# Copies out of the transposes' PSUM banks moved ahead in the engines' queues of an attention and FFN kernel

## The chip, the cores and the metric

The kernel runs on one core of a Trainium2 chip. The metric is the device time of one execution in microseconds (us). Times are medians over several runs; a 95% interval is given where two kernels are compared. Engine names are those of the profile: PE is TensorE's matmuls, PEld its weight loads, DVE is VectorE, ACT is ScalarE, POOL is GpSimd, SP is SyncE. PSUM is the memory that the matmuls and transposes write; its parts are called banks.

## The reference

Attention with a threshold, then an RMS-norm and a gated feed-forward network (FFN). B=8, H=8, S=576, D=64, so 4608 tokens of width 512; d_ff is 1536.

```python
scores = (1/8) * q @ k.T
thresh = scores.max(-1) - tau                     # tau = 0.02
scores = where(scores >= thresh, scores, -1e9)
attn   = softmax(scores)
x      = (attn @ v)                               # heads side by side: 4608 x 512
xn     = x / sqrt(mean(x*x) + 1e-6) * rms_g
out    = (silu(xn @ w_gate) * (xn @ w_val)) @ w_out
```

## The kernel before

The program builds a list of operations and sorts it itself. Each operation has an engine, an assumed cost, a priority number, the operations it depends on, and the PSUM banks it takes or frees. `order_ops` simulates the engines with the assumed costs and fixes the order of every engine's queue when the kernel is built. Among the ready operations of an engine the earliest goes first, and among equals the one with the lower priority number, so **a lower number goes ahead**.

```python
def order_ops(ops, ring_sizes):
    ...
        for e, lst in pending.items():
            ...
            for i in lst:
                o = ops[i]
                t = max(t0, ready_at[i])
                if o.ring is not None:          # banks: wait until o.nring are free
                    free = [f for f in ring_free[o.ring] if ...]
                    if len(free) < o.nring:
                        continue
                    t = max(t, sorted(free)[o.nring - 1][0])
                ...
                k = (t + (BIAS if other else 0.0), o.prio, i)
                if cand is None or k < cand:
                    cand = k
    ...
    seq = order_ops(ops, {"R": 4})
```

Four PSUM banks form the ring `R`. FFN products, attention products and all transposes take their banks from it. A transpose of K and Q (28 sets, two banks each) is emptied by one DVE copy and one ACT copy. Seven transposes of K tails take one bank each, emptied by ACT and then DVE. Four transposes of the last query rows, or query tails, take two banks, both emptied by ACT.

```python
    t = gated(add("PE", COST["tr_qk"], -500.0, ..., tr, ring="R", nring=2, mode=1), prio)
    for r, rs in enumerate(HALF):
        def ev(o, r=r, rs=rs):
            src = ring[t.slot[r]].rearrange("p (j c n) -> p j c n", j=2, n=64)
            if EVAC[r] == "ACT":
                nc.scalar.copy(out=dst[:, :, :, rs], in_=src)
            else:
                nc.vector.tensor_copy(out=dst[:, :, :, rs], in_=src)
        done.append(add(EVAC[r], COST["evac_qk"], prio, [t], ev, frees=(t, r)))
```

What the moved DVE copies pass is the softmax read: it takes the scores of one step out of PSUM (`s_ps`), with the row's extreme. The next score step's matmuls may overwrite `s_ps` only after it. There are 144 score steps, each with two reads of about 0.75 us.

```python
    # the score step: 8 or 16 matmuls into s_ps, waits for the two reads of step s - 1
    for h in range(2):
        deps.append(ttr_of.get((s - 1, h)))
    o = add("PE", COST["s_main" ...], s, deps, fn, ...)

    # the softmax reads of step s
    for h in range(2):
        def ttr(o, h=h):
            nc.vector.tensor_tensor_reduce(
                out=ssb[a][:, h], in0=s_ps[h][:, ROW_AT:ROW_AT + S], in1=zrow, scale=-1.0 / 8.0, scalar=3.0e38,
                op0=ALU.add, op1=ALU.min, accum_out=mx[m][:, h:h + 1])
        ttr_of[s, h] = add("DVE", COST["ttr"], s - 1, [so, o_c] + exp_of.get(s - NSS, []), ttr)
```

FFN blocks are four matmuls `gmm` or `vmm` (gate or value product) that need a bank of the ring, but no softmax result of the score steps around them. They fill PE while the softmax of a step is under way.

## Time and profile before

| | before |
|---|---|
| time, median of the first 3 runs | 564.16 us (564.16 to 564.22) |
| span of the profiled run | 562.9 us |
| PE busy | 553.0 us, 98% |
| ACT, DVE, POOL busy | 459.9, 425.5, 322.5 us |
| granted clock | 0.998, full but for the end |
| ACT copy of K/Q starts after its transposes' end | 1.76 us on average, at most 5.98 |
| DVE copy of K/Q, same | 1.11 us, at most 1.71 |
| ACT copies of query tails, same | 2.21 us, at most 3.41 |

The last three rows are read from the timeline: for every transpose block, the start of its copies less the end of the block. They show what the change goes for: a bank with finished data stands for 1 to 2 us while the copy waits in its queue.

### The profile page before, as it was taken

The numbers are of one execution on the slowest core, as the hardware profiler recorded it, in microseconds if no ns is written. First come the engines' busy times: TensorE is split into PE (matmuls) and PEld (weight loads), VectorE is DVE, ScalarE is ACT, GpSimd is POOL, SyncE is SP. The second block draws the span as 40 slices with busy tenths as digits, with TensorE's granted clock in tenths as the row PEclk, the third lists the DMA queues.
The fourth block names the chain that finished last, engine by engine and source line by source line (L and its number), as shares of the span: only waits on it lengthen the run. The fifth ranks groups of instructions, "written<-read, shape, count | busy, mean of one in ns | idle before, by whom it ended". The sixth has DMA issues, their size and how long they took to land.

```text
span 562.9 us, 15217 instructions
## 1 busy us (share of the span) xinstructions
PE 553.0 (98%) x5768; PEld 315.7 (56%) x5768; DVE 425.5 (76%) x1091; ACT 459.9 (82%) x741; POOL 322.5 (57%) x462
## 2 busy tenths in 40 slices
PE   8899999999999999999999999999999999999997
PEld 4656766757767555545555455545555444444674
DVE  4889987869968589658885889578966886596354
ACT  5999998998989788879888997888989988885332
POOL 2378946985767456665667666666666664551000
PEclk9999999999999999999999999999999999999999
DMA  8999999979986498889887799988898544662210
GB/s 189 259 283 271 159 191 192 193 145 187 202 184 115 111 178 156 181 161 186 151 175 174 122 168 179 181 179 157 171 189 178 116 95 92 151 95 52 85 39 37
DMA packets 270025, 89.08 MB, mean 158 GB/s; under 512 B 252544, under 2 KB 262272, under 8 KB 269952
## 3 DMA queue, kind: packets, MB, share of 16 engines
q1 hardware_dynamic: 267168, 86.02, 75.8%
q0 software_dynamic: 1600, 1.57, 1.8%
q8 instruction: 45, 0.74, 0.6%
q10 hardware_dynamic: 1184, 0.52, 0.3%
q14 instruction: 28, 0.23, 0.2%
HBM read 37.75 MB, written 9.44 MB: 84 GB/s over the span
## 4 chain that ended last, share of the span: by engine, by line
PE 94%; DVE 2%; ACT 1%; DMA 1%; issue 1%; POOL 0%; SPq 0%; DVEq 0%
PE s_ps L569 30%; PE ring L795 17%; PE ring L800 16%; PE ring L856 15%; PE ring L700 6%; PE ring L304 2%; PE ring L696 2%; DVE ssb L592 1%; PE ring L662 1%; PE s_ps L800 1%; PE s_ps L834 1%; PE s_ps L856 1%; DMA stage<-in_q_dram 1%; PE ring L365 1%; PE s_ps L795 0%
## 5 line engine op out<-in xcount | busy, mean ns | idle before, releaser
L592 DVE CUSTOM_DVE_ANT_0 ssb<-s_ps,zrow 128x576 f32<-128x576 f32 x288 | 207.1, 752 | 64.4 <-PE s_ps L569 46.5
L610 ACT ACTIVATE ssb<-ssb,nth 128x576 f32<-128x576 f32 x224 | 166.1, 767 | 27.5 <-POOL nth L599 27.1
L569 PE MATMUL s_ps<-qkt 64*64 64x288 f32 (+1 forms) x1792 | 165.9, 417 | 1.5 <-DVE mx L592 1.5
L643 POOL TENSOR_SCALAR wsb<-ssb,nth 128x576 f16<-128x576 f32 x64 | 110.5, 1726 | 9.7 <-DMA wt<-wsb 3.2
L795 PE MATMUL ring<-xnT,wg 128*128 128x256 f16 (+1 forms) x564 | 114.4, 325 | 0.3 <-DVE xsb L718 0.3
L569 PEld LDWEIGHTS s_ps<-qkt 64*64 64x64 f32 (+1 forms) x1792 | 78.1, 140 | 62.5 <-DVE mx L592 15.5
L800 PE MATMUL ring<-xnT,wv 128*128 128x512 f16 (+1 forms) x528 | 110.4, 331 | 0.0
L599 POOL TENSOR_SCALAR nth<-mx 128x2 f32<-128x2 f32 x144 | 31.7, 220 | 128.1 <-DVE mx L592 118.0
L812 DVE SCALAR_TENSOR_TENSOR sl<-th,ring 128x256 f32<-128x256 f32 (+1 forms) x141 | 77.0, 546 | 30.9 <-ACT th L809 29.6
L617 ACT ACTIVATE wsb<-ssb 128x1152 f16<-128x1152 f32 x80 | 93.0, 1162 | 4.3 <-DMA wt<-wsb 2.2
L809 ACT ACTIVATE th<-ring 128x256 f32<-128x256 f32 (+1 forms) x141 | 67.5, 480 | 29.7 <-PE ring L795 24.7
L856 PE MATMUL ring<-wo,hf 128*128 128x512 f16 x384 | 90.0, 380 | 0.0
L648 POOL TENSOR_TENSOR wsb<-wsb,esb 128x576 f16<-128x576 f16 x64 | 81.8, 1279 | 10.3 <-ACT esb L629 6.0
L817 DVE TENSOR_TENSOR hf<-ring,sl 128x512 f16<-128x512 f32 (+1 forms) x132 | 74.9, 567 | 9.3 <-PE ring L800 0.5
L800 PEld LDWEIGHTS <-wv 128*128 128x128 f16 x576 | 52.2, 98 | 44.5 <-issue 14.2
L795 PEld LDWEIGHTS <-wg 128*128 128x128 f16 x576 | 52.0, 98 | 42.2 <-issue 12.2
L856 PEld LDWEIGHTS <-hf 128*128 128x128 f16 x408 | 37.3, 98 | 47.0 <-issue 7.0
L629 ACT ACTIVATE esb<-ssb,nth 128x576 f16<-128x576 f32 x64 | 49.2, 769 | 6.1 <-POOL nth L599 5.8
L700 PE MATMUL ring<-va,wt 128*128 128x65 f16 (+1 forms) x1264 | 53.0, 193 | 0.0
L700 PEld LDWEIGHTS <-wt 128*128 128x128 f16 (+1 forms) x1280 | 48.8, 100 | 3.8 <-issue 0.7
L614 ACT ACTIVATE wsb<-ssb 128x576 f16<-128x576 f32 x64 | 43.6, 681 | 1.6
L696 PE MATMUL ring<-va,wt 128*128 128x130 f16 (+1 forms) x158 | 35.2, 227 | 0.6 <-ACT qTv L473 0.6
(68 smaller groups left out, 442.3 us busy)
## 6 DMA issues: line engine op xcount, KB each, us to landing
vst<-in_v_dram SPq DMA_DIRECT2D x32, 256.0 KB, 3.7
qkn<-in_k_dram SPq DMA_DIRECT2D x31, 256.0 KB, 3.8
out_dram<-osb SPq DMA_DIRECT2D x31, 256.0 KB, 2.8
qkn<-in_q_dram SPq DMA_DIRECT2D x28, 256.0 KB, 4.3
stage<-in_moe_w_gate_dram SPq DMA_DIRECT2D x6, 512.0 KB, 5.9
stage<-in_moe_w_val_dram SPq DMA_DIRECT2D x6, 512.0 KB, 6.5
wt<-wsb SPq DMA_TRANSPOSE x128, 3.3
wo<-in_moe_w_out_dram POOLq DMA_DIRECT2D x4, 384.0 KB, 6.6
```

The costliest lines, as they stand in the source:

```text
L569: nc.tensor.matmul(s_ps[h][rows, ROW_AT + n * part:ROW_AT + n * part + n], lhs(hs), kT[i][p][h][hs, n * part:n * part + n], start=True, st ...
L592: nc.vector.tensor_tensor_reduce(out=ssb[a][:, h], in0=s_ps[h][:, ROW_AT:ROW_AT + S], in1=zrow, scale=-1.0 / 8.0, scalar=3.0e38, op0=ALU.a ...
L610: nc.scalar.activation(out=ssb[a][:, h], in_=ssb[a][:, h], func=PRELU, scale=-1.0, bias=nth[m][:, h:h + 1], **PRELU_KW)
L617: nc.scalar.activation(out=wsb[s % NW], in_=ssb[a], func=AF.Exp)
L643: nc.gpsimd.tensor_scalar(out=wsb[s % NW][:, h], in0=ssb[a][:, h], scalar1=nth[m][:, h:h + 1], scalar2=None, op0=ALU.is_le)
L648: nc.gpsimd.tensor_tensor(out=wsb[s % NW][:, h], in0=wsb[s % NW][:, h], in1=esb[es], op=ALU.mult)
L700: nc.tensor.matmul(ring[o.slot[0]][rs, at:at + D + 1], w[:, 5 * h + j, rs], va[vi][:, p, 2 * j + h], start=False, stop=(h == 1 and j == 3))
L795: nc.tensor.matmul(ring[o.slot[0]][:, 0:n], wg[d][:, fs], xnT[slot][:, d, 0:n], start=(d == 0), stop=(d == 3))
L800: nc.tensor.matmul(ring[o.slot[0]][:, 0:n], wv[d][:, fs], xnT[slot][:, d, 0:n], start=(d == 0), stop=(d == 3))
L812: nc.vector.scalar_tensor_tensor(out=sl[i][:, 0:n], in0=th[i][:, 0:n], scalar=1.0, in1=ring[g.slot[0]][:, 0:n], op0=ALU.add, op1=ALU.mult)
L817: nc.vector.tensor_tensor(out=hf[hi][:, 0:n], in0=ring[vv.slot[0]][:, 0:n], in1=sl[i][:, 0:n], op=ALU.mult)
L856: nc.tensor.matmul(ring[(first or o).slot[0]], hf[hs[fc][0]][:, 128 * j:128 * (j + 1)], wo[:, fc], start=(fc == 0), stop=(fc == NFC - 1))
```

## The change

Its intent is to give the banks back sooner. The copies' priority numbers go down by 5, 5 and 20 steps, and the first of the two query-tail copies goes from ACT to DVE. No instruction is added or removed. As the priorities feed a list scheduler, any engine's order may come out different, and the changed bank times are among its inputs.

```diff
-            done.append(add(EVAC[r], COST["evac_qk"], prio, [t], ev, frees=(t, r)))
+            done.append(add(EVAC[r], COST["evac_qk"], prio - EVP[0], [t], ev, frees=(t, r)))
...
-            kts.append(add("DVE" if h else "ACT", COST["evac_kt"], prio, [t] + kts, ev, ...))
+            kts.append(add("DVE" if h else "ACT", COST["evac_kt"], prio - EVP[1], [t] + kts, ev, ...))
...
-                nc.scalar.copy(out=qTv[i % 2][:, :, rs],
-                               in_=ring[t.slot[r]][:, 0:64 * NP].rearrange("p (a n) -> p a n", n=64))
+                copy = nc.vector.tensor_copy if not r else nc.scalar.copy
+                copy(out=qTv[i % 2][:, :, rs],
+                     in_=ring[t.slot[r]][:, 0:64 * NP].rearrange("p (a n) -> p a n", n=64))
-            qv_ready[i].append(add("ACT", COST["evac_half"], prio, [t], ev, frees=(t, r)))
+            qv_ready[i].append(add("ACT" if r else "DVE", COST["evac_half"], prio - EVP[2], [t], ev, frees=(t, r)))
...
+EVP = (5.0, 5.0, 20.0)
```

More of the change, by code (lines that the diff above doesn't have):

```diff
@@ L452, in ev @@
                      in_=ring[t.slot[0]][HALF[h], 0:64 * NP].rearrange("p (a n) -> p a n", n=TAIL))
-            kts.append(add("DVE" if h else "ACT", COST["evac_kt"], prio, [t] + kts, ev, frees=(t, 0) if h else None))
+            kts.append(add("DVE" if h else "ACT", COST["evac_kt"], prio - EVP[1], [t] + kts, ev, frees=(t, 0) if h else None))
         for p in range(NP):
```

## The prediction

> **What bounds the kernel now.** I read the page first (busy shares, granted clock), then the busy time by stretch, then the chain of waits in an early and a late stretch, then the waits of TensorE (PE), and last the timeline around every transpose whose copies the change moves.
>
> From the page, and from the table of stretches (columns: stretch, its length, busy us and instructions of each engine, granted clock, DMA share, GB/s):
>
> ```profile
> PE 553.0 (98%) x5768; PEld 315.7 (56%) x5768; DVE 425.5 (76%) x1091; ACT 459.9 (82%) x741; POOL 322.5 (57%) x462
> PEclk9999999999999999999999999999999999999999
> ...
> 14.00:50.00 36.00, 33.43 (x443) 21.91 (x444) 31.74 (x88) 33.21 (x46) 22.21 (x43) 1.00 1.05 272
> 50.00:75.00 25.00, 25.00 (x312) 17.39 (x306) 23.64 (x69) 23.85 (x41) 18.74 (x31) 1.00 1.15 196
> 75.00:150.00 75.00, 74.66 (x935) 48.76 (x930) 60.74 (x172) 67.33 (x117) 52.32 (x71) 1.00 0.97 182
> 150.00:510.00 360.00, 359.43 (x3677) 190.15 (x3674) 277.01 (x684) 310.40 (x486) 224.60 (x304) 1.00 0.79 154
> ```
>
> TensorE is busy nearly always at the full clock. From 150 to 510 us it is busy 359.43 of 360.00 us, with VectorE (DVE) at 77% and ScalarE (ACT) at 86%. Before 75 us DVE and ACT are both close to full as well: 31.74 and 33.21 of 36.00 us, then 23.64 and 23.85 of 25.00.
>
> "Busy" hides slow matmuls, so I checked the pace. In the chain of waits (start us, us, what) a score step, 16 matmuls of L569, looks like this, first early, then late:
>
> ```profile
> 36.65 0.67 DVE ssb L592
> 37.33 0.73 DVE wt L671 x2
> 38.06 0.60 DVE qkt L317
> 38.67 0.08 issue
> 38.75 0.76 DVE ssb L592
> ...
> 42.99 1.87 PE s_ps L569 x16
> ...
> 453.05 1.13 PE s_ps L569 x16
> 454.18 0.97 PE ring L795 x4
> 455.15 0.86 PE ring L800 x4
> 456.01 1.13 PE s_ps L569 x16
> ```
>
> Late, the chain is only TensorE, each score step takes 1.13 us and each FFN block of four 512-column products 0.86, which is 0.216 us a product, back to back. Early, the chain runs through the DVE's softmax reads (L592), its copies of transposed weights (L671) and of transposed K and Q (L317), and a score step stretches to 1.87 us because its second half waits for the reads of the step before.
>
> From the timeline I took for each block of PE instructions the time to the next block's start and subtracted the tenth percentile of blocks of the same kind and successor. The excess, the time in which TensorE is really held up, sums to 15.0 us of 562.9: 0.9 before 14 us, 8.8 from 14 to 75, 3.2 from 75 to 150, 1.5 from 150 to 230, 0.6 from 230 to 510, and nothing in the last 53 us, where the order is FFN work alone. So about 548 us of the span is PE work at its pace. The change leaves that work as it is, and the largest gain that any reordering of copies could have is some 15 us (2.7%), nearly all of it before 230 us.
>
> **What the Trainium skill says.** "PSUM — Partial Sum Buffer", section "Engine vs sequencer instructions", says that the queues of ScalarE and VectorE are strict FIFO. The trace agrees: after the transposes that end at 36.95 us the ACT copy starts 4.43 us later, behind six other ACT instructions, although its data were there. The same page's summary of rules says to evacuate promptly because PSUM is tight; here four banks form the ring that FFN products, attention products and transposes share, and a K/Q transpose holds two. "Perfetto Trace Analysis", section "Identifying the Most-Contended Engine", warns that matmul busy time is not a good measure of the distance to the limit; hence the check of the pace above, which here confirms it after 230 us and refutes it before 75. "VectorE: DVE Perf Modes", section "Why PSUM operands drop a tier", caps fp32 copies from PSUM at one element per cycle, at 0.96 GHz (same page, "Specifications"): 512 elements need at least 0.53 us by it; the trace has 0.685 (L317), and ACT does the same copy in 0.567 (L315).
>
> **The change part by part.** The kernel's order of instructions per engine is fixed at build time by a list scheduler; a lower number goes first among the ready ones of an engine. No instruction is added or removed.
>
> 1. K/Q copies, 28 on DVE and 28 on ACT, move 5 steps forward. In the timeline of before, the DVE copy starts 1.11 us on average after its transposes' end, nearly always behind the two softmax reads (0.75 each); the ACT copy 1.76 us after, at worst 5.98. With 5 steps of lead they go ahead of the reads and exponentials of the current steps. Each pair of banks should come free roughly 0.8 us sooner on DVE (1.11 less about 0.3 for the instruction in hand) and 1.3 on ACT.
> 2. Copies of the K tails, 7 on ACT (0.35) and 7 on DVE (0.43): started 1.32 and 2.40 us after their transposes; both should start within about 0.5 (the DVE one still follows the ACT one).
> 3. Copies of the last query rows: 8 on ACT, 0.36 each, two in a row, started 2.21 us after on average. Four go to DVE at about 0.43 (the duration of the same width in L451). ACT loses 4 x 0.36 = 1.4 us, DVE gains 1.7: too little of 460 and 426 to matter. The pair ends within about 0.8 us instead of 2.6.
>
> What of this lies on the path: only places where PE stood still for such a bank. The waits of PE and the timeline show three.
>
> ```profile
> PE ring L696 <- ACT qTv L473: 0.6, 1, 0.6
> ...
> PE ring L662 <- DVE qkt L317: 0.4, 1, 0.4
> PE ring L795 <- DVE xsb L718: 0.3, 1, 0.3
> ...
> 173.08 0.76 ACT L629 ACTIVATE esb<-ssb,nth 128x576 f16<-128x576 f32 x1
> 173.32 0.10 PEld L696 LDWEIGHTS <-wt 128*128 128x128 f16 x1
> 173.74 0.63 ACT L473 COPY qTv<-ring 128x256 f32<-128x256 f32 x2
> 174.16 0.22 PE L696 MATMUL ring<-va,wt 128*128 128x130 f16 x1 [0.57 <-ACT qTv L473]
> ```
>
> At 174.16 an attention product with its weights loaded waits for the first query-tail copy; at 26.99 a transpose waits for a K/Q copy; at 76.70, with both query-tail banks still held by ACT, an FFN product waits for the one bank left. By the excess of their blocks these cost 0.74, 0.57 and 0.46 us: 1.8 together, and I count all of it as gained.
>
> The other side: a DVE copy ahead of the softmax reads delays them by 0.685, and the next score step waits for those reads. Where FFN blocks can fill, PE loses nothing. Before 50 us there are none: four K/Q transposes and one K tail lie there, so at most 4 x 0.685 + 0.43 = 3.2 us. But the same copy was already on the DVE part of the chain there, only later (38.06 above), so most of it is a swap; I charge a third, 1.1 us.
>
> Third, between 75 and 230 us (4.7 us of excess) free banks let the scheduler put an FFN block where a score step used to follow at once and wait. I count a fifth, 0.9. Sum: -1.8 + 1.1 - 0.9 = -1.6 us, and 564.2 becomes 562.6.
>
> **The rivals.** (a) *Nothing moves*: the held banks are hidden by other work, as PE has no excess from 230 to 510 us although the ACT copy at 295.82 starts 4.06 us late. This speaks for the late part and makes 564. (b) *The delayed softmax becomes the bound*: the scores' reads, then POOL's threshold, then ACT's exponentials all shift by 0.7 to 1.3 us at each of some 13 transposes before 150 us. For it: DVE at 88% and ACT at 92% before 50 us. Against it: later there is filler, and the 20 steps' lead of these inputs is untouched. Charged in full it costs 3.2 before 50 us and perhaps 2 after: 566 to 568. (c) *The banks were the hidden limit early*: free banks let transposes and FFN start sooner and half of the 13.5 us of excess between 14 and 230 us goes: 557. Against it: most of that excess is in score steps that wait for DVE reads, not for a bank.
>
> **Range and chances.** The late 360 us are PE work at full pace and repeat within 0.1 us, so the spread comes from a reshuffled early order: 560.0 to 566.0. Over 2% faster means below 552.9, three quarters of all excess: 0.02. Over 2% slower means 11 us of new stalls in a schedule that has 15: 0.02. Within 2%: 0.96.
>
> **What would show it right or wrong.** The PE wait on L473 at the query tails gone; K/Q copies within about 0.5 us of their transposes on both engines; late score steps still 1.13 us; the busy time from 150 to 510 us of PE unchanged; the score steps before 50 us no longer than now. I am wrong if early score steps lengthen past 1.87 us or PE idles in the waits for L592 more than now (b), if the early stretch shortens by several us (c), or if PE's late order gains switches between its tile shapes and so more work.

## The result and the profile after

The changed kernel takes 564.26 us (563.96 to 565.02, four runs); before, in the same rounds, took 564.19 us (564.16 to 564.23, four runs). The ratio is 1.0003 with a 95% interval of 0.9986 to 1.0021: the same. Ratios here and below are the mean time of one kernel's fast runs over that of the other's of the same rounds, so not quite the ratio of the medians quoted. The profiled spans are 562.3 us after and 562.9 before.

Lines after 473 of the program have moved by one: the score step is now L570, its reads L593, the FFN products L796 and L801, the query-tail copies L474.

The page of the changed kernel: busy us, share and count of each engine.

```profile
PE 550.1 (98%) x5760; PEld 315.2 (56%) x5760; DVE 427.7 (76%) x1095; ACT 458.4 (82%) x737; POOL 322.4 (57%) x462
```

DVE has gained 2.2 us and ACT lost 1.5, mostly the four copies that changed engine. (The eight PE records fewer are of score steps and missing from the trace; no instruction is gone.) PE is busy 2.9 us less, but the span is only 0.6 us shorter. The next view shows where, by stretch, with the columns of the prediction's first fence.

```profile
14.00:50.00 36.00, 32.71 (x440) 22.07 (x438) 31.68 (x90) 32.70 (x46) 21.84 (x43) 1.00 1.08 273
50.00:75.00 25.00, 24.50 (x304) 16.99 (x301) 23.34 (x67) 23.66 (x40) 19.45 (x31) 1.00 1.12 205
75.00:150.00 75.00, 74.04 (x933) 49.70 (x933) 61.24 (x173) 67.35 (x117) 51.92 (x70) 1.00 0.93 173
150.00:510.00 360.00, 359.21 (x3630) 188.62 (x3632) 277.90 (x680) 304.74 (x476) 219.65 (x298) 1.00 0.78 152
```

PE has gaps of 0.7, 0.5, 0.6 and 0.2 us more than before in these four stretches; what it waits for comes below. From 150 to 510 us there are fewer PE instructions in the same busy time (3630 against 3677), and ACT has 5.7 us less to do there: attention's small matmuls and exponentials have moved later, and larger FFN products have come forward. The last softmax read ends at 516.0 us, against 507.0 before, and 960 of the FFN's 1152 first-layer matmuls (four make a block) have begun before it, against 920. The order of work on PE is a different one.

The chain of waits in a late stretch (start us, us, what) answers to the prediction's second fence:

```profile
440.06 1.13 PE s_ps L570 x16
441.19 0.97 PE ring L796 x4
442.16 0.86 PE ring L801 x4
```

The pieces are what they were: 1.13, 0.97 and 0.86 us. The waits of PE (who waited for whom, total us, times, longest):

```profile
PE ring L663 <- ACT wsb L618: 2.4, 3, 1.6
...
PE ring L796 <- DMA xnT<-xn: 0.6, 1, 0.6
PE s_ps L570 <- DVE mx L593: 0.5, 2, 0.3
...
PE ring L801 <- DVE qkt L317: 0.4, 1, 0.4
...
PE ring L796 <- DVE qkt L317: 0.3, 1, 0.3
PE ring L801 <- ACT qkt L315: 0.2, 1, 0.2
```

No wait for a query-tail copy is left. The largest entry is new: at 34.63, 47.92 and 50.93 us (0.32, 1.59 and 0.50 us) the transposes of attention weights wait for ACT's exponentials, a wait that before does not have. It is 2.4 of the 3.8 us that PE stands from 14 to 75 us. FFN products now wait for K/Q copies in three places, although the copies come sooner, because FFN blocks now stand right behind transposes. One wait is for the FFN's own input, `xnT`: at 478.79 us FFN work has run so far ahead that its transposed input has not landed. And in the timeline, at the query tail of 172 us (start us, us, engine, line, operation):

```profile
171.75 0.41 PE L463 MATMUL ring<-id,qtl 64*128 64x64 f32 x8
...
172.19 0.42 DVE L474 COPY qTv<-ring 128x256 f32<-128x256 f32 x1
172.23 0.37 ACT L474 COPY qTv<-ring 128x256 f32<-128x256 f32 x1
```

The two copies now run side by side and end 0.45 us after the transposes (172.61 less 172.16). The change does to the copies what it was meant to: mean delays are 0.37 us on DVE and 0.34 on ACT for K/Q, and 0.32 and 0.25 for the query tails.

**A finer measure.** For the comparison below I took again, for each block of PE instructions, the time from its start to the next block's start, and subtracted the tenth percentile of blocks of the same kind and successor. This time the percentiles are pooled over four kernels: before, after and two experiments, x3_hoist and z1_act_only, which come below. The sum of the percentiles is "work", the rest "excess"; together they fall 7.6 to 7.8 us short of the span in all four kernels. With pooling, the excess of before is 18.1 us instead of the prediction's 15.0.

| us | work | excess | of it 0-14 | 14-75 | 75-150 | 150-230 | from 230 |
|---|---|---|---|---|---|---|---|
| before | 537.2 | 18.1 | 2.6 | 9.4 | 3.4 | 1.6 | 1.1 |
| after | 537.1 | 17.4 | 2.0 | 9.5 | 3.3 | 0.9 | 1.7 |
| x3_hoist | 537.1 | 24.4 | 2.5 | 9.7 | 5.1 | 3.5 | 3.7 |
| z1_act_only | 537.2 | 18.2 | 2.7 | 9.1 | 3.4 | 1.9 | 1.1 |

PE's work has not changed, and neither has its excess, but for a few tenths that come and go. So the new waits for exponentials before 51 us stand in place of other losses there: the net from 14 to 75 us is 0.1.

### The profile page after: what moved, and what is told of

Read it like the earlier page. It is cut to its first block, busy times and chain, and to the rows that moved or that the text cites. A ratio compares the mean times of both kernels' runs of the same rounds, so it can differ in the third digit from the quotient of the medians.

```text
span 562.3 us, 15189 instructions
## 1 busy us (share of the span) xinstructions
PE 550.1 (98%) x5760; PEld 315.2 (56%) x5760; DVE 427.7 (76%) x1095; ACT 458.4 (82%) x737; POOL 322.4 (57%) x462
## 4 chain that ended last, share of the span: by engine, by line
PE 86%; DVE 4%; ACT 3%; DMA 2%; issue 2%; POOL 1%; SPq 1%; DVEq 0%; POOLq 0%
PE s_ps L570 26%; PE ring L801 17%; PE ring L796 17%; PE ring L857 14%; PE ring L701 6%; DVE ssb L593 2%; PE ring L304 2%; PE ring L697 2%; ACT ssb L611 1%; PE s_ps L835 1%; PE s_ps L857 1%; DMA qkn<-in_q_dram 1%; DMA qkn<-in_k_dram 1%; DMA xnT<-xn 1%; PE ring L663 1%
## 5 line engine op out<-in xcount | busy, mean ns | idle before, releaser
L593 DVE CUSTOM_DVE_ANT_0 ssb<-s_ps,zrow 128x576 f32<-128x576 f32 x288 | 208.6, 752 | 71.9 <-PE s_ps L570 56.0
L570 PE MATMUL s_ps<-qkt 64*64 64x288 f32 (+1 forms) x1784 | 163.1, 417 | 0.7 <-DVE mx L593 0.5
L796 PE MATMUL ring<-xnT,wg 128*128 128x512 f16 (+1 forms) x552 | 113.9, 329 | 1.2 <-DMA xnT<-xn 0.6
L801 PE MATMUL ring<-xnT,wv 128*128 128x512 f16 (+1 forms) x552 | 113.8, 329 | 0.6 <-DVE qkt L317 0.4
L570 PEld LDWEIGHTS s_ps<-qkt 64*64 64x64 f32 (+1 forms) x1784 | 77.3, 140 | 59.4 <-issue 14.1
L813 DVE SCALAR_TENSOR_TENSOR sl<-th,ring 128x512 f32<-128x512 f32 (+1 forms) x138 | 76.6, 555 | 19.2 <-ACT th L810 18.0
L810 ACT ACTIVATE th<-ring 128x512 f32<-128x512 f32 (+1 forms) x138 | 67.1, 487 | 26.2 <-PE ring L796 23.4
L818 DVE TENSOR_TENSOR hf<-ring,sl 128x512 f16<-128x512 f32 (+1 forms) x138 | 77.6, 562 | 11.7 <-DVE sl L813 0.9
L801 PEld LDWEIGHTS <-wv 128*128 128x128 f16 x576 | 53.0, 98 | 42.5 <-issue 12.1
L796 PEld LDWEIGHTS <-wg 128*128 128x128 f16 x576 | 51.6, 98 | 44.2 <-issue 13.5
```

Of the source, the lines that this page charges most:

```text
L570: nc.tensor.matmul(s_ps[h][rows, ROW_AT + n * part:ROW_AT + n * part + n], lhs(hs), kT[i][p][h][hs, n * part:n * part + n], start=True, st ...
L593: nc.vector.tensor_tensor_reduce(out=ssb[a][:, h], in0=s_ps[h][:, ROW_AT:ROW_AT + S], in1=zrow, scale=-1.0 / 8.0, scalar=3.0e38, op0=ALU.a ...
L796: nc.tensor.matmul(ring[o.slot[0]][:, 0:n], wg[d][:, fs], xnT[slot][:, d, 0:n], start=(d == 0), stop=(d == 3))
L801: nc.tensor.matmul(ring[o.slot[0]][:, 0:n], wv[d][:, fs], xnT[slot][:, d, 0:n], start=(d == 0), stop=(d == 3))
L813: nc.vector.scalar_tensor_tensor(out=sl[i][:, 0:n], in0=th[i][:, 0:n], scalar=1.0, in1=ring[g.slot[0]][:, 0:n], op0=ALU.add, op1=ALU.mult)
L818: nc.vector.tensor_tensor(out=hf[hi][:, 0:n], in0=ring[vv.slot[0]][:, 0:n], in1=sl[i][:, 0:n], op=ALU.mult)
```

## The experiments

The copies start a microsecond sooner at 39 transposes, and the time stays. Two theories stood at first. **H (hidden)**: the banks were hardly wanted by anyone, so nothing gained and nothing lost. **C (cancel)**: the earlier copies cost something, and something else of about the same size is won. The first four runs do one part of the change, or its opposite.

**e1_qk_only**: only the K/Q copies go ahead; query tails stay on ACT.

```diff
-EVP = (5.0, 5.0, 20.0)
+EVP = (5.0, 0.0, 0.0)
-            qv_ready[i].append(add("ACT" if r else "DVE", ...))
+            qv_ready[i].append(add("ACT", ...))             # and nc.scalar.copy for both
```

> Only the 56 K/Q copies go ahead by 5 steps; K tails and query tails as before. Theory A (TensorE's fixed work sets the time, banks were hidden): within 1 us of 564.2. Theory B (two effects of 1 to 3 us cancel: copies ahead of the softmax cost time early, query tails on two engines win it back): 565 to 567 here, with the loss between 14 and 75 us.

Measured: 573.64 us (571.34 to 575.97) against 564.76, ratio 1.0156 (1.0119 to 1.0193). Slower by 9 us, so H can't be all. Part of it is the clock. The four runs order themselves by it: 571.34 us at a mean granted clock of 1.000, 573.34 at 0.997, 573.93 at 0.996 and 575.97 at 0.994. The stretches of its trace around the dip (columns as above; the third number from the end, ahead of the DMA share, is the granted clock):

```profile
78.00:83.00 5.00, 3.47 (x58) 2.36 (x50) 3.15 (x10) 4.64 (x9) 1.77 (x4) 1.00 0.83 151
83.00:87.00 4.00, 4.00 (x40) 2.10 (x37) 2.33 (x7) 2.52 (x6) 3.67 (x5) 0.57 1.25 244
```

PE stood 1.53 of 5 us, in three waits: 0.38 us at 80.45 for a bank, 0.42 at 81.47 for a late query-tail copy and 0.73 at 82.66 for a DMA of attention weights. From 83.14 us it had half the clock for 3.41 us, which costs about half of that, 1.7 us. That the waits caused it is not shown, as no run takes them away alone. The run at full clock is still 6.6 us slower; where some of that lies comes under y1_qk_and_qt.

**e3_qt_only**: only the query tails, on two engines.

```diff
-EVP = (5.0, 5.0, 20.0)
+EVP = (0.0, 0.0, 20.0)
```

> Only the 8 copies of the last query rows: on two engines, 20 steps ahead. Theory A: within 1 us of 564.2, the wait of PE on the query-tail copy (0.57 us at 174 us) gone, at most 0.7 us gained. Theory B: 562 to 563.

Measured: 563.44 us (562.81 to 563.54) against 564.76, ratio 0.9974 (0.9959 to 0.9989). PE's wait of 0.57 us for the query tail is gone in its trace, and no other has come. This is the one kernel whose interval lies below 1, by 1.3 us in the medians.

**e4_behind**: the opposite, every one of these copies 5 steps later, query tails on ACT.

```diff
+EVP = (-5.0, -5.0, -5.0)
```

> The other way: all these copies go 5 steps behind instead of ahead, so banks stay held longer (1 to 3 us more per transpose). Theory A (banks are hidden by other work after 75 us): under 2 us slower, 564 to 566. Rival C (banks are the hidden limit, and the kernel before already sat where it no longer shows): 4 us or more slower.

Measured: 569.95 us (568.78 to 571.61), ratio 1.0094 (1.0075 to 1.0114). The ACT copies of K/Q started 2.73 us after their transposes on average (1.76 before), at worst 11.2; those of K tails started 3.6 and 4.8 us late, at worst 15 to 16, and those of query tails 5.0. So the opposite of the change costs some 5 us. Whether the longer held banks cost it or the new order that came with them is not shown, as no run delays the copies in a fixed order. By a pooling of its own, about half lies in PE's work and half in excess between 50 and 150 us.

**e6_later_batches**: as after, but the copies of the first two batches (numbers 0 and 1) as before.

```diff
-            done.append(add(EVAC[r], COST["evac_qk"], prio - EVP[0], ...))
+            done.append(add(EVAC[r], COST["evac_qk"], prio - (EVP[0] if b > 1 else 0.0), ...))   # K tails alike
```

> The change, except that batch 1, whose transposes lie before 50 us, keeps its old order. Theory A: within 1 us of 564.2 again. Theory B: the early loss is gone and the query tails' gain stays: 561.5 to 563.

Measured: 563.96 us, ratio 1.0001 (0.9973 to 1.0030; one run took 567.42 at a clock of 0.996). The early copies, on which the prediction spent its charge, make no difference that these runs show.

**How much does a new order do by itself?** A part of the change, like the change, lets the scheduler make a new order. Two runs measure what a meaningless reshuffle does: the scheduler's assumed cost of one operation goes from 800 to 810, which changes no instruction and puts most rows of PE's queue elsewhere.

```diff
-    ... sq=800.0, ...
+    ... sq=810.0, ...
```

**n2_null** is this on before, **n4_null** on after.

> A null change to the kernel before: the scheduler is told that one ACT instruction, the square of the norm, takes 810 ns, not 800; the instructions are the same and no priority changes, but the order of most PE rows does. Theory D: differs from before by up to several us in either direction (2 to 8 us), as e1 and e4 do. Theories A and B, where priorities of copies are what matters: within 1 us of before.

> The same null change to the changed kernel. Theory D: differs from the changed kernel by several us; a spread of 562 to 572 among orders. Theories A and B: within 1 us of the changed kernel, 564.3.

Measured: n2_null 563.39 us against 564.20, ratio 0.9985 (0.9968 to 1.0001); n4_null 564.10, ratio 0.9997 (0.9982 to 1.0012). These two reshuffles moved the time by 0.8 and, against after in other rounds, 0.2 us. The 6.6 us and more of e1 and the 5 of e4 are well outside that, though two reshuffles are a small sample, and e3's gain of 1.3 us is barely larger than what a meaningless edit gave.

**Copies early, everything else in place.** To part the copies from the new order, the schedule of before is kept and the copies alone are moved forward afterwards in their own queues, to where their transposes' data are ready in the scheduler's model.

**x1_hoist** and **x2_hoist_two** (the second with the first query-tail copy on DVE):

```diff
+    for c, t in early:
+        seq.remove(c)
+        ready = max(d.end for d in c.deps) + SEM
+        at = seq.index(t) + 1
+        while at < len(seq) and not (seq[at].eng == c.eng and seq[at].start >= ready):
+            at += 1
+        seq.insert(at, c)
```

> The schedule of before is kept: PE, POOL and DMA queues in exactly the order of before; only the copies (K/Q, K tails, query tails, the last still both on ACT) are taken forward in the DVE and ACT queues to where their transposes end. Theory A (banks cost 1.8 us at three places and an early softmax delay of about 1 us is paid): 562.5 to 565, copies start under 0.6 us after their transposes. Theory D (what moves the time by several us in e1 and e4 is not the copies but the new order that the scheduler makes of everything else): also within 1.5 us of before. Theory B (copies ahead of the softmax cost several us): 567 or more.

> As x1, and the first of each two query-tail copies on DVE: the whole change without a new plan. Theory A: as the changed kernel, 562.5 to 565, the wait at 174 us gone. Theory D: within 1.5 us of x1 and of before.

Measured: 571.66 and 573.0 us, but both gave **wrong results** (relative error 0.478). The loop could put a copy behind its old place, past the next use of its bank. Their times say nothing. The mended version never goes past the old place:

**x3_hoist**, with the query tails on ACT, and **x4_hoist_two**, with the first of them on DVE:

```diff
+    for c, t in early:                  # (copy, its transposes), noted where the copies are added
+        was = seq.index(c)
+        ready = max(d.end for d in c.deps) + SEM
+        at = seq.index(t) + 1
+        while at < was and seq[at].start < ready:
+            at += 1
+        seq.pop(was)
+        c.start, c.end = ready, ready + c.cost
+        seq.insert(at, c)
```

> x1 mended (there a copy could land later than it had been, behind a reuse of its bank, hence the wrong result; both x1 and x2 say nothing on time). PE, POOL and DMA queues in the order of before; the copies only ever move forward, to where their transposes end, the query tails' both on ACT. Theory A (copies as such are worth little either way): 562.5 to 566, copies start under 0.7 us after their transposes on average. Theory B (copies ahead of the softmax cost several us): 567 or more. If it is near before, the 9 us of e1 come from the order that was planned around the copies, not from the copies.

> x2 mended: as x3, with the first of each two query-tail copies on DVE; the whole change, without a new plan of everything else. Theory A: within 1 us of x3 and at most 0.7 us better, as the wait at 174 us goes. If the plan is what the change is worth, x4 is slower than the changed kernel (564.3) by 0.5 us or more; if the copies are, equal to it.

Measured: x3_hoist 570.98 us (570.80 to 571.38) against 564.63, ratio 1.0111 (1.0096 to 1.0126), with right results; x4_hoist_two 571.99, ratio 1.0128 (1.0113 to 1.0143). In x3_hoist the queues of PE, POOL and SP are row for row those of before, and the copies' delays are those of after: 0.37 us on DVE and 0.40 on ACT. Nothing but the place of the copies differs, and it costs 6.3 us. The table above has all of it in the excess (24.4 against 18.1), and all but 0.2 after 75 us. By kind of block it is all in the score steps: after 14 us their excess is 15.9 us in x3_hoist and 9.5 in before (counted afresh, with blocks cut a little differently).

The mechanism can be read off one transpose. The same K/Q transposes of batch 3, in the timeline of before:

```profile
141.46 0.66 PE L304 MATMUL ring<-id,qkn 64*128 64x64 f32 x16
...
142.34 0.75 DVE L592 CUSTOM_DVE_ANT_0 ssb<-s_ps,zrow 128x576 f32<-128x576 f32 x1
...
142.58 1.76 PE L569 MATMUL s_ps<-qkt 64*64 64x288 f32 x16
...
143.59 0.69 DVE L317 COPY qkt<-ring 128x512 f32<-128x512 f32 x1
```

and in that of x3_hoist, where the score step is L574, its read L597 and the DVE copy L319 (in brackets: PE's idle time before, and what ended it):

```profile
143.75 0.69 DVE L319 COPY qkt<-ring 128x512 f32<-128x512 f32 x1
...
143.89 0.69 PE L574 MATMUL s_ps<-qkt 64*64 64x288 f32 x2
...
144.35 0.75 DVE L597 CUSTOM_DVE_ANT_0 ssb<-s_ps,zrow 128x576 f32<-128x576 f32 x1
...
145.16 1.19 PE L574 MATMUL s_ps<-qkt 64*64 64x288 f32 x14 [0.58 <-DVE mx L597]
```

Before, the second read runs right behind the first and the copy comes last; the score step's second half has to wait a little (1.76 us for a step that this view shows at 1.20 when nothing holds it). In x3_hoist the copy sits between the two reads; the second half of the score step stands 0.58 us for the second read, and the step ends 2.46 us after it began (146.35 less 143.89) instead of 1.76. And in that of after:

```profile
143.65 0.61 PE L796 MATMUL ring<-xnT,wg 128*128 128x256 f16 x4
...
143.88 0.69 DVE L317 COPY qkt<-ring 128x512 f32<-128x512 f32 x1
...
144.48 0.75 DVE L593 CUSTOM_DVE_ANT_0 ssb<-s_ps,zrow 128x576 f32<-128x576 f32 x1
...
144.62 0.60 PE L801 MATMUL ring<-xnT,wv 128*128 128x256 f16 x4 [0.35 <-DVE qkt L317]
...
145.05 0.60 PE L796 MATMUL ring<-xnT,wg 128*128 128x256 f16 x4
145.58 1.20 PE L570 MATMUL s_ps<-qkt 64*64 64x288 f32 x16
```

Here the copy sits between the reads just as in x3_hoist, and the second read is as late. But the scheduler has put three FFN blocks between the transposes and the score step. When the step starts, the reads are done, and it takes 1.20 us. Over the 24 K/Q transposes after 75 us, before and x3_hoist have 1.29 FFN blocks (of either layer) between a transpose's end and the next score step, after has 1.96. The mean score step of 16 matmuls, from its start to the next block's, is from 75 to 150 us 1.25 us in before, 1.35 in x3_hoist and 1.19 in after; from 150 to 230 us 1.17, 1.31 and 1.14.

PE's waits for the reads say the same. In before:

```profile
PE s_ps L569 <- DVE mx L592: 1.5, 4, 0.4
```

and in x3_hoist:

```profile
PE s_ps L574 <- DVE mx L597: 3.2, 9, 0.6
```

From 1.5 us they double to 3.2 with the order of before, and fall to 0.5 in after's.

**y1_qk_and_qt**: the full change without the K tails' part, as a test of whether K/Q copies need company.

```diff
-EVP = (5.0, 5.0, 20.0)
+EVP = (5.0, 0.0, 20.0)
```

> e1 and e3 together: K/Q copies 5 steps ahead, query tails on two engines 20 ahead, K tails as before. If e1 lost its 9 us because K/Q copies pushed the query tails' copies further back on ACT (3.17 us after their transposes, from 2.21) and a bank wait at 82 us set off the drop of the clock: 563 to 566 here. If the K tails, still behind while their neighbours went ahead, were the cause: 570 or more.

Measured: 569.31 us (569.11 to 570.81) against 564.63, ratio 1.0089 (1.0071 to 1.0107). So whether the seven K tails move with the rest decides some 5 us. This is not the loss of x3_hoist over again: y1 has 1.92 FFN blocks behind a transpose, and its mean score steps are 1.17 us from 75 to 150 us and 1.15 from 150 to 230, no longer than after's. PE's waits for the reads are 3.0 us in its trace, as in x3_hoist, but 1.3 us of them come after 475 us. Its late order shows a place where filler ran out (timeline of PE alone):

```profile
475.62 1.90 PE L570 MATMUL s_ps<-qkt 64*128 64x288 f32 x8
478.01 1.87 PE L570 MATMUL s_ps<-qkt 64*64 64x288 f32 x16 [0.50 <-DVE mx L593]
```

Two score steps follow each other with no FFN block between, and the second starts 2.39 us after the first. The same happens again at 480.86 us. Each pair takes 4.2 us up to the next block, where the two steps at their pace take 2.2 (1.07 for 8 matmuls, 1.13 for 16), so the two pairs make up about 4 of the 5 us. e1_qk_only has two such pairs as well, at 480.90 and 485.95 us; before, after, x3_hoist and z1_act_only have none. They lie where after, too, is short of FFN work (its wait for `xnT` at 478.79 us). So the new order is not always a good one: by these traces, FFN work that is brought forward is missing at the end of attention, which no run tries by itself. Why it runs out with K tails left behind and not with them ahead, I did not settle.

**z1_act_only**: as x3_hoist, but only the ACT copies move, which leaves DVE's queue, PE's, POOL's and SP's exactly as before. This tells whether it is the banks, the ACT side or the DVE side.

```diff
     for c, t in early:
+        if c.eng != "ACT":
+            continue
```

> x3 with only the copies on ACT taken forward; PE, POOL, DMA and also DVE in the order of before. x3 lost 6.3 us, all of it in score steps that wait for the DVE's softmax reads (L592). If a DVE copy ahead of these reads is the cause: within 1.5 us of before here (563 to 566), the waits of the score steps on those reads as before (about 17 us of weight loads). If the ACT copies ahead of the exponentials hold up the softmax and through its buffers the reads: 568 or more. In between: both share it.

Measured: 564.81 us (564.63 to 565.12) against 564.38, ratio 1.0004 (0.9987 to 1.0020). ACT's K/Q copies come 0.31 us after their transposes instead of 1.76, and the time stays. Putting copies ahead of exponentials on ACT costs nothing here, and having those banks a microsecond sooner gains nothing with PE's order as it was. The weight loads of the score steps wait 18.0 us for the softmax reads here, 17.4 in before and 22.3 in x3_hoist. As x3_hoist less z1_act_only is the DVE copies alone, **some 6 us are theirs**: 28 K/Q copies of 0.685 us and 7 of K tails, put in front of the softmax reads. (DVE copies ahead with the ACT copies left in place were not run.)

Neither theory holds as first put. H is right for the banks on ACT at fixed order (z1_act_only). C is right for the whole: the copies cost 6.3 us in a fixed order (x3_hoist), nearly all of it by those on DVE, or some 7.4 with the query tail on two engines (571.99 less 564.63), and the scheduler's new order takes about as much back. The last is shown by the step from x4_hoist_two to after: the same copies on the same engines, as early, differ in the order of the queues, and 572.0 becomes 564.3 (7.4 and 0.1 us above before of the same rounds). *What* in the new order does it, the FFN blocks between transposes and score steps, is read from the traces and was not tried by itself.

## Why the prediction was right or wrong

The time was predicted at 562.6 us, between 560.0 and 566.0, and it is 564.26. The arithmetic behind it held only in part.

| step | predicted | measured |
|---|---|---|
| K/Q copies sooner, DVE and ACT | 0.8 and 1.3 us | 0.74 and 1.42 us |
| K-tail copies start after | about 0.5 us on both | 0.13 us on ACT, 1.10 on DVE |
| pair of query-tail copies ends after | about 0.8 us | 0.79 us on average |
| three waits for banks | -1.8 us | about -1.1 there, and three new ones for K/Q copies of 0.8 together |
| delayed reads before 50 us | +1.1 us | at most 0.1 over 14 to 75 us |
| 75 to 230 us | -0.9 us | -0.8 us, of which 0.6 is given back after 230 |
| sum | -1.6 us | -0.6 us of span, +0.07 in the timed medians |

The measured rows overlap, as the places of the fourth row lie in the stretches of the next two, so they don't add up to the last; the excess adds up in the table of stretches above: -0.6 before 14 us, +0.1, -0.1, -0.7 and +0.6.

**The copies** did as foreseen, but for the DVE copies of K tails: each waits for the ACT copy of its tail, 0.35 us long, and the soonest starts 0.59 us after the transposes. The checks on the late part held: a score step of 1.13 us and 359.21 us of PE busy time where there had been 359.43. So did the one on rival (b): PE waits 0.5 us for the reads, not 1.5, and the score steps from 14 to 50 us are no longer than before (1.67 us on average in both).

**The three bank waits** are the term that was mis-sized. At 174 us the wait is gone (0.74). At 27 us the wait fell from 0.57 to about 0.25. At 76 us a wait of 0.46 remains: the bank that the FFN product needs there is held by another copy, `xsb`, so that the query-tail copies were only one of two that had to end. In exchange FFN products wait for K/Q copies at three places, 0.35, 0.27 and 0.21 us, where FFN work now follows a transpose more closely. I had counted all removed waits as gained and no new one; the 2.4 us for exponentials before 51 us and the 0.6 for `xnT` are new as well. z1_act_only shows the general form of it: banks freed sooner on ACT at 28 transposes gain nothing while PE's order stays.

**The charge for delayed reads** rested on the step "Where FFN blocks can fill, PE loses nothing", and put all of it before 50 us. With the order of before this is wrong in its place and its size: x3_hoist loses 6.3 us, nearly all after 75 us and some 4.5 of it after 150, just where there *is* filler, because the order that is fixed at build time doesn't use it at these places. The early stretch, which I charged, loses at most 0.3. It came out true of the changed kernel only because the scheduler planned again and moved filler to the transposes. Rival (b), 566 to 568 us, was therefore a real effect and even larger than I had put it, 571 at a fixed order, and my only line for the re-plan that pays for it was the third step, 0.9 us. That the total was near is luck: two terms of six to eight us, which I had put at 1.1 and 0.9, cancel.

**The third step**, free banks letting FFN blocks in between 75 and 230 us, named what the trace shows, FFN blocks at these places, and -0.8 us is the net there. That free banks let them in is not shown: z1_act_only frees banks on ACT, but keeps PE's order. And it was not kept to the end: FFN work ran 40 matmuls, or 10 blocks, ahead, at 478.79 us it waited 0.58 us for its own input, and attention ended 9 us later.

Also not foreseen: after's four runs spread over 1.06 us, before's over 0.07. The spread was predicted to come "from a reshuffled early order". e6_later_batches, with the early copies as before, does not show less, so where it comes from stays open.

## What to carry to other kernels

A bank that is held too long costs only where somebody waits for it, and a copy put at the head of a queue that runs strictly in order takes its time from whatever stood there: ask which of the two has the next matmul behind it. Where a scheduler plans from priorities, test a change of priority twice, with the plan frozen and with the plan made anew, since the two can differ by more than the change is worth, and measure what a meaningless reshuffle does before believing one microsecond. Filler that is moved forward is missing later: look for the place where it runs out. Here the best found is the smallest part, the query tails alone at 563.44 us, and even that is 0.3%.

## What the Trainium skill lacked or had wrong

- "PSUM — Partial Sum Buffer", summary of rules for kernel authors, says to evacuate promptly. It lacks the price: copies put ahead on both engines cost 6.3 us in an unchanged order (x3_hoist), and the same done to the ACT copies alone changed the time by 0.04%, inside its interval (z1_act_only). The rule needs "unless the queue's next entry is what the matmuls wait for".
- "TensorE: Matmul & The Clock Gate", section "HAM oscillation — how this bites in real kernels", gives the rule that PE must not idle for longer than about 3.4 us at a time. In e1_qk_only the clock was halved for 3.41 us after PE had stood 1.53 of 5 us, with no wait longer than 0.73 us. That rule does not cover it. The page goes on to tell of frequent short idle times that also lower the clock, but gives no figure for how much idle time is enough. That these waits caused the dip is not shown here.
- No page read for this says that an order fixed at build time is an input of its own: a change of 10 ns in one assumed cost, with no instruction changed, put another row at 3605 of the 5768 places of PE's queue (n2_null) and gave a median 0.8 us lower, though the interval of the ratio still reaches 1 (0.9968 to 1.0001).
